# Slot experts fed by layers: two tiles cleared late on other engines, domain weights normalized ahead, two dense tiles fetched last, low parts by halves

## The chip, the cores and the metric

One NeuronCore of a Trainium2 chip runs the whole program. The metric is device time of one execution in microseconds (us), the median of three runs. Five engines work beside each other, each with its own in-order queue: PE (TensorE, matrix products), DVE (VectorE), ACT (ScalarE), POOL (GpSimd) and SP (SyncE), which here only issues DMA transfers. An instruction waits on semaphores for what it needs, and everything behind it in the same queue waits with it.

## What is computed

Three stages, one after the other. Inputs and outputs are float32; B, H, S, D = 4, 8, 576, 64; x has 2304 rows of 512.

```python
def _attn_ref(q, k, v, f):
    scores = scale * np.matmul(q, k.transpose(0, 1, 3, 2))
    cum = np.cumsum(np.log(np.clip(f, 0.0001, 1.0)), axis=-1)
    scores = np.where(causal, -1e9, scores + cum[:, :, :, None] - cum[:, :, None, :])
    attn = softmax(scores)                       # over the last axis
    return np.matmul(attn, v)

def _moe_ref(x, phi, w1, w2):                    # 8 experts of 4 slots
    logits = x @ phi
    d = softmax(logits, axis=0); c = softmax(logits, axis=1)
    slot_input = d.T @ x
    for e in range(E):
        slot_out[e] = np.maximum(slot_input[e] @ w1[e], 0.0) @ w2[e]
    return c @ slot_out

def _moe2_ref(x, domain_probs, w1, w2):          # 4 dense experts, 512 -> 1024 -> 512
    p = domain_probs / (domain_probs.sum(-1, keepdims=True) + 1e-09)
    for e in range(E):
        out += p[:, e:e + 1] * (np.maximum(x @ w1[e], 0.0) @ w2[e])
    return out
```

## The kernel before, in words

**Stages.** Attention and the sums of the slot softmax run to about 212 us of the trace. Then come the eight slot experts in two layers: layer 1 (L762) for all experts, layer 2 (L787) expert by expert into one PSUM tile `so_ps`, with the last expert done in two halves of 256 columns (`layer2_last`, L797 and L799). Then `so_t`, the transposed slot output (L982, L983), is multiplied with the first dense layer of expert 0 (`g_make`, L959, split into a high part `gh` and a low part `gl` at L965 and L966), is spread over the slots (L872, L873), and from there the dense stage begins: for each of 36 blocks (4 experts x 9 pairs of row tiles), PE combines 512 hidden values with `c4t` (L887), ACT and DVE build the pieces `q`, `a` and sums `S`, and PE multiplies them with the second layer. Block m=0 does this directly (L1079). The other 35 blocks (L1059) use a Strassen scheme with seven products in place of eight.

**High and low parts.** Products in the dense stage are made from a rounded high part and a low part. The weights of one expert are four blocks B00, B10, B01, B11 and four sums T1 to T4 of them (L733). Each has a high part, cast by ACT (L746, `w_hi`), and a low part, the difference of the source and the high part (L752, `w_lo`), by POOL or DVE. Each is 128x1024, in four pieces of 256 columns; `0:2` and `2:4` name the halves. The pieces S have low parts too (L953, on POOL). The products of PE use them in the order high x high, low x high, high x low.

**Queues.** In attention a scheduler places the instructions. From the slot experts on, the order of PE, ACT, DVE and POOL is the order in which the code is written (`manual_schedule`). The order of the dense stage's preparations for expert 0 stands in the table `PRE0`, keyed by block and step. SP's queue carries all loads in one order (`load_w` takes the next of a list `stream`); eight transfers are in flight, since a transfer waits for the one eight before it. A weight tile is 128x1024 float32, 512 KB. The second dense layer of expert 0 is a buffer of four such tiles, called `ring` (`load_ring`); the four tiles of its first layer are called `m`, the slot experts' tiles `w`.

**Small tiles that the change touches.** `own` is a mask of ones (expert's own slots), used at L778; `si_f` holds the slot inputs, filled at L665; both are cleared by POOL at L168 to L170, when the program starts. `dpr` holds the domain probabilities, loaded by SP at L834; DVE normalizes it into `dpn` at L1019 to L1022, through `dps` (128x18), right behind the pieces of block m=0. `sel` (128x1024, a selector) is cleared and filled by POOL at L844 and L848. `c4_rep` (L694 to L697) makes for each of five `b` a rounded copy `chi`, a spread copy and a difference of `cn`, all on POOL. `orow` are the two halves of the last rows of `so_ps`, copied by ACT at L976.

Of the kernel before, what the change touches and what calls it, by code (L numbers as in the profile page):

```python
# [34 lines left out]
def soft_moe_kernel(tc, a, out):  # L35
# [12 lines left out]
    with ExitStack() as top:  # L48
# [104 lines left out]
        own = tl.tile([128, E1 * 36], F32, name="own")  # L153
# [405 lines left out]
        load_w(ex.enter_context(tc.tile_pool(name="post", bufs=6)), 6)  # L559

# [12 lines left out]
        with tc.manual_schedule(engines={E.PE, E.Activation, E.DVE}):  # L573
# [56 lines left out]
            dnat(B - 1)  # L630
            busy(1)
# [37 lines left out]
            pool.tensor_tensor(cn[:, B - 1], ce, cs[:, :, None].to_broadcast([128, 5, 32]), op=ALU.mult)  # L669

# [16 lines left out]
        c4_ps = {}  # L687

        def c4_rep(b):
# [3 lines left out]
            chi = c4p.tile([r, 4, 32], F32R, tag="chi", bufs=2, name=f"chi_{b}")  # L693
            pool.tensor_scalar(chi, src, 1.0, 1.0, op0=ALU.mult, op1=ALU.mult)  # L694
            two_of = lambda x: x[:, :, None, :].to_broadcast([r, 4, 2, 32])
            pool.tensor_scalar(c4[:, :, 0:4:2], two_of(f32(chi)), 1.0, 1.0, op0=ALU.mult, op1=ALU.mult)
            pool.tensor_tensor(c4[:, :, 1:4:2], two_of(src), two_of(f32(chi)), op=ALU.subtract)  # L697
            c4_ps[b] = c4

# [105 lines left out]
        for e in range(E1):  # L805
# [462 lines left out]
```

## Time and profile before

| quantity | value |
|---|---|
| median of three runs | 665.27 us (664.82 to 665.33) |
| the profiled execution, its own time | 666.66 us |
| span of its trace | 664.9 us |
| PE busy | 651.0 us, 98% of the span |
| DVE, ACT, POOL busy | 495.5, 348.8, 424.0 us (75%, 52%, 64%) |
| mean DMA rate over the span | 115 GB/s |

The span is what the trace covers of the profiled execution; 1.76 us of its time lie outside. In the page's strip of 40 slices (16.6 us each) PE has a 7 in the first slice and an 8 in the last and otherwise nines, with a few eights in the first third; the strip of the granted TensorE clock has one 7, in the slice from 266 to 283 us, and nines around it. So PE does almost nothing but work, and what can be looked for are the places where it waits, and what the clock does behind them. The engines beside it have a quarter and more of their time free, but the average says nothing on a given stage.

### The profile page before, as it was taken

What the parts mean: (1) busy time and instruction counts of PE and PEld (TensorE: products, weight loads), DVE (VectorE), ACT (ScalarE), POOL (GpSimd) and SP (SyncE); (2) the same over time, 40 slices, a digit from 0 to 9 for tenths busy, and PEclk for the clock granted to TensorE, in tenths of its full rate; (3) what the DMA queues carried; (4) which work ended last, traced back from release to release, by engine and by line L of the source; (5) the groups of instructions that cost most, each with busy time, mean ns of one, the idle gap of its engine ahead of it and who ended that gap; (6) DMA issues with size and microseconds to landing.
All of it is one profiled execution on the core that took longest, in us unless ns stands there. A gap on an engine that the chain in (4) does not pass through costs nothing.

```text
span 664.9 us, 15324 instructions
## 1 busy us (share of the span) xinstructions
PE 651.0 (98%) x5646; PEld 583.4 (88%) x5646; DVE 495.5 (75%) x1332; ACT 348.8 (52%) x840; POOL 424.0 (64%) x402
## 2 busy tenths in 40 slices
PE   7999999999999989899999999999999999999998
PEld 4778778788787439899999999999999999999997
DVE  6888889889884147867678876778876778876774
ACT  6778767777771135333547343447443446443441
POOL 5777767777641199453889663789753589835443
PEclk8999999999999999799999999999999999999999
DMA  5778687686247980303000303000303000011111
GB/s 167 227 219 252 187 271 219 205 275 184 85 166 303 414 334 1 127 1 129 1 1 1 128 1 127 2 0 2 128 1 128 1 1 2 33 48 48 52 45 64
DMA packets 27509, 76.15 MB, mean 115 GB/s; under 512 B 4014, under 2 KB 4654, under 8 KB 27436
## 3 DMA queue, kind: packets, MB, share of 16 engines
q1 hardware_dynamic: 27436, 75.18, 33.1%
q8 instruction: 45, 0.74, 0.5%
q14 instruction: 28, 0.23, 0.1%
HBM read 70.31 MB, written 4.72 MB: 113 GB/s over the span
## 4 chain that ended last, share of the span: by engine, by line
PE 86%; DVE 6%; DMA 4%; ACT 2%; issue 2%; DVEq 0%; ACTq 0%; SPq 0%
PE R L1059 28%; PE Q L1059 14%; PE P L1059 7%; PE pt L273 5%; PE avb L290 5%; PE two L887 5%; PE sc L240 3%; PE sc L237 3%; PE sc L224 3%; PE pl L342 2%; PE ava L302 2%; PE pt L264 2%; DMA m<-in_m 1%; DMA w<-in_w 1%; DVE dps L1020 1%
## 5 line engine op out<-in xcount | busy, mean ns | idle before, releaser
L953 POOL TENSOR_TENSOR s<-S,s 128x512 fp32r<-128x512 f32 x140 | 179.8, 1318 | 141.7 <-ACT s L949 141.7
L949 ACT CAST s<-S 128x512 fp32r<-128x512 f32 x140 | 77.1, 619 | 96.0 <-PE Q L1059 52.0
L214 ACT ACTIVATE p<-p,nm 128x256 f32<-128x256 f32 (+2 forms) x144 | 83.4, 580 | 28.4 <-DVE nm L210 27.1
L1059 PE MATMUL R<-wh_T,s 128*128 128x256 f32 x560 | 89.2, 281 | 0.6 <-DVE acc L1042 0.6
L1042 DVE SCALAR_TENSOR_TENSOR acc<-R,dpn,acc 128x256 f32<-128x256 f32 x116 | 56.0, 482 | 37.4 <-PE R L1059 34.2
L919 ACT ACTIVATE a<-two 128x256 f32<-128x256 f32 x70 | 26.9, 384 | 97.5 <-PE two L887 97.0
L1059 PEld LDWEIGHTS R<-wh_T,s 128*128 128x128 f32 x560 | 75.9, 188 | 1.4 <-ACT a L928 1.1
L210 DVE CUSTOM_DVE_ANT_0 p<-sc,maskb 128x256 f32<-128x256 f32 (+2 forms) x144 | 67.1, 489 | 4.2 <-PE sc L224 1.4
L945 DVE SCALAR_TENSOR_TENSOR S<-two,S 128x256 f32<-128x256 f32 x140 | 58.9, 420 | 3.6 <-POOL s L953 1.1
L945 DVE SCALAR_TENSOR_TENSOR S<-two,a 128x256 f32<-128x256 f32 x140 | 58.1, 415 | 0.0
L191 POOL TENSOR_TENSOR opd<-raw,opd 64x576 fp32r<-64x576 f32 x29 | 42.6, 1468 | 14.4 <-ACT opd L176 13.3
L237 PE MATMUL sc<-opd 128*128 128x256 f32 (+3 forms) x128 | 47.0, 377 | 1.6 <-ACT opd L509 1.6
L1059 PE MATMUL R<-wh_B,a 128*128 128x256 f32 x280 | 45.3, 284 | 3.1 <-DVE acc L1040 3.1
L935 DVE SCALAR_TENSOR_TENSOR q<-two,q 128x512 fp32r<-128x512 f32 x70 | 47.7, 681 | 0.0
L273 PE MATMUL pt<-ident,p 128*128 128x128 f32 x285 | 46.7, 282 | 0.5 <-DVE ptb L178 0.5
L887 PE MATMUL two<-c4t,gs 128*128 128x256 f32 x288 | 46.9, 286 | 0.0
L1059 PE MATMUL P<-wh_B,q 128*128 128x256 f32 x280 | 45.1, 283 | 0.0
L1059 PE MATMUL R<-wh_T,q 128*128 128x256 f32 x280 | 44.8, 282 | 0.0
L1059 PE MATMUL Q<-wh_T,s 128*128 128x256 f32 x280 | 44.4, 280 | 0.0
L1059 PE MATMUL R<-wl_T,s 128*128 128x256 f32 x280 | 44.3, 280 | 0.0
L1059 PE MATMUL Q<-wh_B,s 128*128 128x256 f32 x280 | 44.3, 280 | 0.0
L273 PEld LDWEIGHTS pt<-ident,p 128*128 128x128 f32 x285 | 32.1, 143 | 13.7 <-issue 10.3
(272 smaller groups left out, 1641.5 us busy)
## 6 DMA issues: line engine op xcount, KB each, us to landing
w<-in_w SPq DMA_DIRECT2D x54, 512.0 KB
ring<-in_m SPq DMA_DIRECT2D x28, 512.0 KB
raw<-in_k SPq DMA_DIRECT2D x64, 144.0 KB
v<-in_v SPq DMA_DIRECT2D x16, 320.0 KB
out<-acc SPq DMA_DIRECT2D x17, 256.0 KB
raw<-in_q SPq DMA_DIRECT2D x28, 144.0 KB
ring<-in_w SPq DMA_DIRECT2D x4, 512.0 KB
w_opd<-in_w SPq DMA_DIRECT2D x4, 512.0 KB
```

Source lines behind the costliest of these rows:

```text
L191: (dve if h == 0 else pool).tensor_tensor(lo, r, f32(hi), op=ALU.subtract)
L210: dve.tensor_tensor_reduce(out=pt_in[j][:, k0:k0 + n], in0=sc, in1=maskb[:, m0:m0 + n], scale=-SCALE, scalar=nm, op0=ALU.add, op1=ALU.min, ...
L214: act.activation(p, p, AF.Exp, bias=nm, scale=-1.0, accum_out=sums)
L237: pe.matmul(o, lhsT=qa[hh][:, qs], rhs=ka[hh][:, 0:n], start=True, stop=False)
L273: pe.transpose(t[:, i, :], pt_in[j][:, 128 * i:128 * i + 128], ident)
L887: pe.matmul(t[:, j, k], lhsT=gs[e][:, 128 * fc:128 * fc + 128], rhs=c4t[:, nb * BLK:nb * BLK + BLK])
L935: dve.scalar_tensor_tensor(o[:, 1], i, 0.0, f32(o[:, 0]), op0=ALU.max, op1=ALU.subtract)
L945: dve.scalar_tensor_tensor(sv[m, name][:, c], half[m, h][:, :, k, 128 * t:128 * t + 128], 0.0, other, op0=ALU.max, op1=op)
L949: act.copy(tile_of(m, name)[:, 0], sv[m, name])
L953: (eng or pool).tensor_tensor(o[:, 1], sv[m, name], f32(o[:, 0]), op=ALU.subtract)
L1042: dve.scalar_tensor_tensor(o, t, pcol, o, op0=ALU.mult, op1=ALU.add)
L1059: pe.matmul(t, lhsT=a[:, c, :], rhs=w[:, c, :], start=first and x == 0 and c == 0, stop=x == 2 and c == 3, skip_group_check=True)
```

## The change

1. `si_f` is cleared by ACT, at the end of the softmax (L632 of the changed kernel), and `own` (now bfloat16) by DVE behind L670, rather than both by POOL at the start.
2. `dpn` is loaded during attention and normalized in place, at L672 to L675, between the slot softmax and the slot experts, rather than inside block m=0.
3. The tiles of the second dense layer of expert 0 are no longer fetched together ahead of the last slot experts' tiles: two (chunks 0 and 2, which hold the halves 0:2) keep their place, the other two (chunks 1 and 3) go last, behind the four `m` tiles.
4. The high and low parts of B00 to B11 and T1 to T4 are made by halves: `0:2` as soon as the first two tiles are there, `2:4` later (partly between the steps of blocks 0 and 1, table `PRE0`). All low parts are POOL's now; DVE's four are gone.
5. `sel` is cleared and filled by ACT, and ACT makes the two copies of `c4_rep`; POOL keeps the difference (`c4_low`).

The diff, cut to its core:

```diff
-        pool.memset(own, 0.0)
-        pool.memset(own.rearrange("p (e x) -> p e x", x=36)[:, :, 0:4], 1.0)
-        pool.memset(si_f, 0.0)
...
+        sp.dma_start(out=dpn, in_=a["dp"])
...
             dnat(B - 1)
+            act.activation(si_f, ident[:, 0:1].to_broadcast([128, E1 * 132]), AF.Copy, scale=0.0)
...
             dve.reciprocal(cs, cs)
             pool.tensor_tensor(cn[:, B - 1], ce, cs[:, :, None].to_broadcast([128, 5, 32]), op=ALU.mult)
+            dve.tensor_reduce(dps, dpn, axis=AX.X, op=ALU.add)
+            dve.tensor_scalar(dps, dps, 1e-9, None, op0=ALU.add)
+            dve.reciprocal(dps, dps)
+            dve.tensor_tensor(dpn, dpn, dps[:, :, None].to_broadcast([128, 18, E2]), op=ALU.mult)
+            dve.memset(own, 0.0)
+            dve.memset(own.rearrange("p (e x) -> p e x", x=36)[:, :, 0:4], 1.0)
...
-            chi = c4p.tile([r, 4, 32], F32R, tag="chi", bufs=2, name=f"chi_{b}")
-            pool.tensor_scalar(chi, src, 1.0, 1.0, op0=ALU.mult, op1=ALU.mult)
+            chi = c4p.tile([r, 4, 32], F32R, tag="chi", bufs=5, name=f"chi_{b}")
+            act.copy(chi, src)
...
-            pool.tensor_scalar(c4[:, :, 0:4:2], two_of(f32(chi)), 1.0, 1.0, op0=ALU.mult, op1=ALU.mult)
-            pool.tensor_tensor(c4[:, :, 1:4:2], two_of(src), two_of(f32(chi)), op=ALU.subtract)
+            act.copy(c4[:, :, 0:4:2], two_of(f32(chi)))
...
+            c4_in[b] = (c4[:, :, 1:4:2], two_of(src), two_of(f32(chi)))
+        def c4_low(b):
+            pool.tensor_tensor(*c4_in[b], op=ALU.subtract)
...
             if e == 0:
-                raws[0] = load_ring(stream.index(("m2", 0, 0)))
+                raws[0] = ring.tile([128, 4096], F32, tag="w", name="ring_m2")
+                for i in (0, 2):
+                    load_w(raws[0][:, 1024 * i:1024 * i + 1024], 1, stream.index(("m2", 0, i)))
             elif e < 6:
                 load_w(ringb[0], 4 if e < 5 else 1)
+            if e == 5:
+                for i in (1, 3):
+                    load_w(raws[0][:, 1024 * i:1024 * i + 1024])
...
-            w_sum(0, x, 2, 4)
-        pool.memset(f32(sel), 0.0)
+        for x in ("B00", "B10", "B01", "B11"):
+            w_hi(0, x, act, 0, 2)
+            w_lo(0, x, pool, 0, 2)
+        slots(5)
+        layer2(5)
+        w_hi(0, "T2", act, 0, 2)
+        w_hi(0, "T1", act, 0, 2)
+        for b in (0, 1, 2, 3, B):
+            c4_rep(b)
+        act.activation(sel, ident[:, None, None, 0:1].to_broadcast([128, 4, 2, 128]), AF.Copy, scale=0.0)
         for jq in range(4):
             for i in range(2):
...
-        w_hi(0, "B00", act)
-        w_hi(0, "B10", act)
-        w_lo(0, "B00", dve, 0, 2)
-        slots(5)
-        layer2(5)
-        w_hi(0, "B01", act)
-        w_hi(0, "B11", act)
-        w_hi(0, "T2", act)
-        w_hi(0, "T1", act)
-        for b in (0, 1, 2, 3, B):
-            c4_rep(b)
-        w_lo(0, "B00", dve, 2, 4)
+        c4_low(0)
+        w_sum(0, "T3", 0, 2)
+        w_sum(0, "T4", 0, 2)
...
         slots(6)
-        w_lo(0, "B10", dve, 0, 2)
         slots(7)
-        w_lo(0, "B10", dve, 2, 4)
...
+        w_hi(0, "B00", act, 2, 4)
+        w_lo(0, "B00", pool, 2, 4)
...
-        dve.tensor_reduce(dps, dpr, axis=AX.X, op=ALU.add)
-        dve.tensor_scalar(dps, dps, 1e-9, None, op0=ALU.add)
-        dve.reciprocal(dps, dps)
-        dve.tensor_tensor(dpn, dpr, dps[:, :, None].to_broadcast([128, 18, E2]), op=ALU.mult)
...
+        PRE0 = {(0, 0): [("hi", "B01", "a", 2, 4), ("lo", "B01", "p", 2, 4)],
```

What the diff doesn't tell is how the queues read afterwards. In the rows of an order the first word is the line of that kernel, then operation, tiles (out<-in) and size.

SP's queue of loads, before: the four ring tiles together, then the w tiles of the last slot experts (`w2`, left out in part), then the m tiles (`m1`), then the probabilities.

```order
L73 DMA w2_4_2_3250<-in_w2 128x1024
L73 DMA ring_45_3284<-in_m2 128x1024 x4
L73 DMA w2_4_3_3305<-in_w2 128x1024
L73 DMA w2_5_0_3307<-in_w2 128x1024
...
L73 DMA w2_7_3_3379<-in_w2 128x1024
L73 DMA m1_0_0_3381<-in_m1 128x1024
L73 DMA m1_0_1_3383<-in_m1 128x1024
L73 DMA m1_0_2_3385<-in_m1 128x1024
L73 DMA m1_0_3_3409<-in_m1 128x1024
L834 DMA dpr_3507<-in_dp 128x72
```

SP's queue there now:

```order
L73 DMA w2_4_2_3258<-in_w2 128x1024
L73 DMA ring_m2_3292<-in_m2 128x1024 x2
L73 DMA w2_4_3_3311<-in_w2 128x1024
L73 DMA w2_5_0_3313<-in_w2 128x1024
...
L73 DMA w2_7_3_3385<-in_w2 128x1024
L73 DMA m1_0_0_3387<-in_m1 128x1024
L73 DMA m1_0_1_3389<-in_m1 128x1024
L73 DMA m1_0_2_3391<-in_m1 128x1024
L73 DMA m1_0_3_3415<-in_m1 128x1024
L73 DMA ring_m2_3292<-in_m2 128x1024 x2
```

Each w and m tile stands two transfers further ahead, and two ring tiles stand at the end.

DVE's queue where block m=0 ends and block m=1 begins, before: the four operations on `dps` and `dpn` stand between the pieces `q` and the sums `S`.

```order
L898 SCALAR_TENSOR_TENSOR q1_0_3713<-two1_3260,q1_0_3713 128x512
L898 SCALAR_TENSOR_TENSOR q2_0_3716<-two1_3260,q2_0_3716 128x512
L1019 TENSOR_REDUCE dps_3508<-dpr_3507 128x18
L1020 TENSOR_SCALAR dps_3508<-dps_3508 128x18
L1021 RECIPROCAL dps_3508<-dps_3508 128x18
L1022 TENSOR_TENSOR dpn_3505<-dpr_3507,dps_3508 128x72
L945 SCALAR_TENSOR_TENSOR S1_1_3818<-two0_3259,a21_1_0_3794 128x256
L945 SCALAR_TENSOR_TENSOR S2_1_3820<-two0_3259,S1_1_3818 128x256
```

They stand now at the end of the slot softmax, ahead of the slot experts:

```order
L667 TENSOR_TENSOR si_f_132<-maskb_97,busy_2_3194 128x8x2x4
L669 TENSOR_SCALAR cs_e_3199<-cs_e_3199 128x5
L670 RECIPROCAL cs_e_3199<-cs_e_3199 128x5
L672 TENSOR_REDUCE dps_135<-dpn_134 128x18
L673 TENSOR_SCALAR dps_135<-dps_135 128x18
L674 RECIPROCAL dps_135<-dps_135 128x18
L675 TENSOR_TENSOR dpn_134<-dpn_134,dps_135 128x72
L676 MEMSET own_133 128x144
L677 MEMSET own_133 128x8x4
```

Behind the `q` of block m=0 the sums `S` follow at once.

POOL's queue in blocks 0 and 1 now, from the second halves on (before, L752 and L733 stood there for whole blocks, and two of the eight low parts were made by DVE):

```order
L763 TENSOR_TENSOR wl_0_B11_3544<-ring_m2_3292,wh_0_B11_3543 128x512
L744 TENSOR_TENSOR T1_0_3527<-ring_m2_3292 128x512
L744 TENSOR_TENSOR T2_0_3529<-T1_0_3527,ring_m2_3292 128x512
L744 TENSOR_TENSOR ring_m2_3292<-ring_m2_3292 128x2x256
L744 TENSOR_TENSOR ring_m2_3292<-ring_m2_3292,T2_0_3529 128x2x256
L763 TENSOR_TENSOR wl_0_T2_3558<-T2_0_3529,wh_0_T2_3557 128x512
L763 TENSOR_TENSOR wl_0_T1_3561<-T1_0_3527,wh_0_T1_3560 128x512
L968 TENSOR_TENSOR s0_1_3912<-S2_1_3828,s0_1_3912 128x512
L968 TENSOR_TENSOR s0_1_3912<-S1_1_3826,s0_1_3912 128x512
L763 TENSOR_TENSOR wl_0_T3_3618<-ring_m2_3292,wh_0_T3_3617 128x512
L968 TENSOR_TENSOR s1_1_3937<-S3_1_3849,s1_1_3937 128x512
L968 TENSOR_TENSOR s1_1_3937<-S4_1_3851,s1_1_3937 128x512
```

The low parts of block 1's sums (`s0_1`, `s1_1`) now stand behind the second halves of all weights. The order of loads and of POOL's work inside attention also differs, by some places, since the scheduler placed it anew with two memsets less; PE's order there is the same.

## Rows read from the trace of the kernel before

**Rows 1.** Waits of PE, whole span: us in total, times, longest.

```profile
PE R L1059 <- DVE acc L1040: 3.1, 1, 3.1
PE two L797 <- DMA w<-in_w: 1.8, 3, 0.6
...
PE two L959 <- DMA m<-in_m: 0.5, 1, 0.5
...
PE sc L240 <- DMA opd<-opd: 0.3, 1, 0.3
```

**Rows 2.** Windows: us, busy of PE, PEld, DVE, ACT, POOL (count), granted clock, DMA share, GB/s.

```profile
212.00:226.00 14.00, 13.94 (x251) 8.19 (x254) 0.86 (x3) 0.38 (x1) 0.45 (x1) 1.00 0.88 349
...
238.00:248.00 10.00, 7.71 (x88) 3.36 (x80) 1.84 (x5) 1.23 (x3) 9.44 (x20) 1.00 0.83 335
...
252.40:265.00 12.60, 12.56 (x106) 12.36 (x104) 11.23 (x6) 6.52 (x13) 12.60 (x11) 1.00 0.00 1
265.00:268.00 3.00, 0.00 (x0) 0.00 (x0) 2.90 (x10) 0.00 (x0) 0.15 (x1) 0.88 0.00 0
268.00:272.00 4.00, 3.92 (x18) 3.95 (x19) 3.97 (x10) 2.18 (x5) 1.48 (x2) 0.50 0.02 4
272.00:275.00 3.00, 3.00 (x20) 3.00 (x19) 1.13 (x4) 1.04 (x3) 3.00 (x3) 0.65 0.26 57
```

**Rows 3.** DVE's timeline: start us, us, line, operation; in brackets the idle time before.

```profile
211.91 0.19 DVE L668 RECIPROCAL cs_e<-cs_e 128x5 f32<-128x5 f32 x1
...
232.83 1.29 DVE L752 TENSOR_TENSOR wl_B<-ring,wh_B 128x512 fp32r<-128x512 f32 x1
...
236.17 0.68 DVE L752 TENSOR_TENSOR wl_B<-ring,wh_B 128x512 fp32r<-128x512 f32 x1
...
243.46 0.42 DVE L799 TENSOR_TENSOR orow<-orow,two 128x256 f32<-128x256 f32 x1 [4.91 <-PE two L797]
...
248.40 0.42 DVE L965 CAST gh<-two 128x256 fp32r<-128x256 f32 x1 [2.54 <-PE two L959]
...
256.39 8.79 DVE L1020 TENSOR_SCALAR dps<-dps 128x18 f32<-128x18 f32 x1
```

**Rows 4.** POOL's timeline, same columns.

```profile
229.81 2.52 POOL L733 TENSOR_TENSOR T<-ring 128x512 f32<-128x512 f32 x2 [17.11 <-PE so_ps L787]
...
236.25 2.90 POOL L848 TENSOR_SCALAR sel<-i 32x64 fp32r<-32x64 f32 x8
...
239.99 0.73 POOL L697 TENSOR_TENSOR c<-cn,chi 128x256 f32<-128x256 f32 x1
...
256.39 5.03 POOL L752 TENSOR_TENSOR wl_T<-T,wh_T 128x512 fp32r<-128x512 f32 x4
261.38 3.77 POOL L752 TENSOR_TENSOR wl_T<-ring,wh_T 128x512 fp32r<-128x512 f32 x3
```

**Rows 5.** PE's timeline from the last slot expert to the dense stage.

```profile
241.46 0.63 PE L797 MATMUL two<-w,ht 128*32 128x256 f32 x4 [0.61 <-DMA w<-in_w]
242.71 1.49 PE L797 MATMUL two<-w,ht 128*32 128x256 f32 x20 [0.62 <-DMA w<-in_w]
244.13 0.63 PE L982 MATMUL two<-i,orow 128*128 128x32 f32 x4
...
245.53 1.66 PE L959 MATMUL two<-m,so_t 128*32 128x256 f32 x24
247.69 0.64 PE L959 MATMUL two<-m,so_t 128*32 128x256 f32 x8 [0.51 <-DMA m<-in_m]
```

**Rows 6.** Chain of waits, 222 to 247 us: start us, us, what.

```profile
237.73 9.92 DMA m<-in_m
```

**Rows 7.** ACT's timeline, 226 to 249 us.

```profile
231.48 3.89 ACT L746 CAST wh_B<-ring 128x1024 fp32r<-128x1024 f32 x4 [4.38 <-DMA w<-in_w]
235.81 2.00 ACT L746 CAST wh_T<-T 128x1024 fp32r<-128x1024 f32 x2 [0.44 <-issue]
239.29 0.65 ACT L976 COPY orow<-so_ps 128x256 f32<-128x256 f32 x2 [1.48 <-PE so_ps L787]
```

More of the change, by code (lines that the diff above doesn't have):

```diff
@@ L152, in soft_moe_kernel @@
         si_f = tl.tile([128, E1 * 132], F32, name="si_f")
-        own = tl.tile([128, E1 * 36], F32, name="own")
+        own = tl.tile([128, E1 * 36], BF16, name="own")
+        dpn = tl.tile([128, 18, E2], F32, name="dpn")
+        dps = tl.tile([128, 18], F32, name="dps")
+        tl.tile([128, 46], F32, name="pad")
         si_t = si_f.rearrange("p (e x) -> p e x", x=132)[:, :, 0:128].rearrange("p e (c y) -> p e c y", y=32)[:, :, :, 0:4]
@@ L685, in soft_moe_kernel @@
         ops = top.enter_context(tc.tile_pool(name="ops", bufs=4, space=PSUM))
-        c4_ps = {}
+        c4_ps, c4_in = {}, {}
         def c4_rep(b):
@@ L829, in soft_moe_kernel @@
         so_t = c4tp.tile([128, DC, 32], F32, name="so_t")
-        dpn = c4tp.tile([128, 18, E2], F32, name="dpn")
         sel = c4tp.tile([128, 4, 2, 128], F32R, name="sel")
-        dpr = c4tp.tile([128, 18, E2], F32, name="dpr")
-        dps = c4tp.tile([128, 18], F32, name="dps")
-        sp.dma_start(out=dpr, in_=a["dp"])
+        c4tp.tile([128, 8], F32, name="pad2")
         gsp = top.enter_context(tc.tile_pool(name="gsp", bufs=2, side="right"))
@@ L847, in soft_moe_kernel @@
                 r = slice(32 * jq, 32 * jq + 32)
-                pool.tensor_scalar(sel[r, jq, i, 64 * i:64 * i + 64].rearrange("p (a s) -> p a s", a=2),
-                                   i4[r, None, :].to_broadcast([32, 2, 32]), 1.0, 1.0, op0=ALU.mult,
-                                   op1=ALU.mult)
-        w_hi(0, "B00", act)
-        w_hi(0, "B10", act)
-        w_lo(0, "B00", dve, 0, 2)
-        slots(5)
-        layer2(5)
-        w_hi(0, "B01", act)
-        w_hi(0, "B11", act)
-        w_hi(0, "T2", act)
-        w_hi(0, "T1", act)
-        for b in (0, 1, 2, 3, B):
-            c4_rep(b)
-        w_lo(0, "B00", dve, 2, 4)
+                act.copy(sel[r, jq, i, 64 * i:64 * i + 64].rearrange("p (a s) -> p a s", a=2),
+                         i4[r, None, :].to_broadcast([32, 2, 32]))
+        c4_low(0)
+        w_sum(0, "T3", 0, 2)
+        w_sum(0, "T4", 0, 2)
+        c4_low(1)
+        c4_low(2)
+        w_lo(0, "T2", pool, 0, 2)
+        c4_low(3)
+        c4_low(B)
+        w_lo(0, "T1", pool, 0, 2)
         slots(6)
-        w_lo(0, "B10", dve, 0, 2)
         slots(7)
-        w_lo(0, "B10", dve, 2, 4)
         def g_spread(e, gh, gl, hf):
@@ L976, in soft_moe_kernel @@
             act.copy(orow[h], so_ps[:, 256 * h:256 * h + 256])
+        for x in ("T3", "T4"):
+            w_hi(0, x, act, 0, 2)
+            w_lo(0, x, pool, 0, 2)
         for h in range(2):
@@ L991, in soft_moe_kernel @@
             c4_hi(b)
-        for x in ("B01", "B11"):
-            w_lo(0, x, pool, 0, 2)
-            w_lo(0, x, pool, 2, 4)
-        for x in ("T3", "T4"):
-            w_sum(0, x, 0, 2)
-            w_sum(0, x, 2, 4)
         attn.close()
@@ L1003, in soft_moe_kernel @@
             g_spread(0, *gg, hf)
+        w_hi(0, "B10", act, 2, 4)
+        w_lo(0, "B10", pool, 2, 4)
         c4_tr(3, c4_bank(3))
@@ L1097, in soft_moe_kernel @@
                (9, 4): [("lo", "B11", "p", 2, 4), ("lo", "T4", "d", 0, 2)], (9, 5): [("lo", "T4", "p", 2, 4)]}
-        PRE0 = {(0, 0): [("lo", "T2", "p", 0, 2)], (0, 1): [("hi", "T3", "a", 0, 4), ("lo", "T2", "p", 2, 4)],
[3 rows of a table removed]
+        PRE0 = {(0, 0): [("hi", "B01", "a", 2, 4), ("lo", "B01", "p", 2, 4)],
[6 rows of a table added]
         ENG = {"a": act, "d": dve, "p": pool}
```

9 rows, old and new, of the table PRE0 are left out of this document.

## The prediction, on record before the changed kernel ran

> **What bounds the kernel now.** I read PE's waits over the whole span first [rows 1]. PE is busy for 98% of it, and what it waits for by name is small, with two exceptions: once 3.1 us for DVE (L1040), and 1.8 + 0.5 us for DMA of the slot experts' tiles w and of the dense tiles m. Both lie between 238 and 275 us, so the windows of that stretch come next [rows 2]. The reader is to see three things there. From 238 to 248 PE works 7.71 of 10 us. From 265 to 268 it does nothing. Behind that its granted clock is 0.50 (the 1.2 GHz level) for 4 us and 0.65 on average for 3 more, while it is busy throughout: work goes on at half speed.
>
> The DMA wait is read from PE's timeline [rows 5]: L797 starts at 241.46 and 242.71 as w tiles land, 1.24 us apart, and L959 waits once more for the last m tile, which lands at 237.73 + 9.92 = 247.65 [rows 6]. All transfers stand in one stream at its full rate, so the order in the queue decides what lands when.
>
> The DVE wait is read from its timeline [rows 3]: the tensor_scalar on `dps`, 18 numbers a partition, takes 8.79 us, 256.39 to 265.18, where the reciprocal of five numbers takes 0.19. Beside it POOL runs seven low parts without a gap and ends at 261.38 + 3.77 = 265.15 [rows 4]. DVE is let go when POOL stops. The sums S and the copies to `acc` of block m=0 stand behind it on DVE; PE needs those banks, and waits 3.1 us.
>
> **The change part by part.**
>
> *dps out of block m=0.* The loss is the idle time and what the lower clock cost. Of the 10 us from 265 to 275, PE did work worth 4 x 0.50 + 3 x 0.65 = 3.95 us at full clock [rows 2], so 6.05 us are lost. Afterwards q of block m=0 ends at about 256.2 on DVE, S follows at once, and nothing that I see is late before PE gets there: at most 3 us of DVE work stand between q and the start of block m=1. Gain 6.05, if nothing else takes the place (rival 1). The four operations now run at about 212.1, behind the reciprocal that ends there [rows 3]. POOL runs one instruction of 0.45 us in that whole stage [rows 2]; even shut out by it they end near 213.3, as do the two clears of `own`, whose first reader is layer 2. PE enters layer 1 on `si_f` and its own products, both ahead of them. Cost nothing; without that cover it would be about 1 us.
>
> Here a page bears on it. The Trainium skill, SBUF — State Buffer, section "Who interferes with whom", says that DVE and POOL share a port pair as an exclusive lock held for one whole instruction, and that DVE needs it in a 2-port mode or with two inputs in SBUF. That agrees with a tensor_scalar that can't run beside POOL; but by that rule it would wait for one POOL instruction, 5.03 / 4 = 1.26 us, dps would not be what is late, and the time would be that of rival 3. The trace shows it shut out for seven in a row [rows 3, 4], and the row decides.
>
> *Ring order.* Two tiles fewer stand ahead of each w and m tile: 2 x 1.24 = 2.48 us earlier. The last w tile lands at 240.23 rather than 242.71, the last m tile at 245.17; the two late ring tiles at 246.4 and 247.65. That would be worth 2.48 us if nothing else came last.
>
> *What is late next: ACT.* `layer2_last` adds to `orow`, which ACT copies from `so_ps`; before, ACT was free and did so at 239.29 [rows 7]. Now it has ahead of this: four casts 128x512 from 231.48, two more from 235.81 (when T1, T2 and the queue allow it in the trace of before), five pairs of `chi` and c4 copies, the clear of `sel` and eight small copies. From rows: 3.89 / 4 = 0.97 for 1024 columns and 0.65 / 2 = 0.33 for 256 give 0.5 to 0.55 for 512, 0.3 for each of the ten copies, 0.97 to 1.05 for the clear. That is 236.9 behind T1 and T2, 240.0 behind the copies, 241.0 behind the clear; for the eight 32x64 copies I take 0.17 each (0.33 less 192 columns at (0.97 - 0.33) / 768 a column; bounds, as estimates, 0.15 and 0.25), so 242.3, and `orow` at 242.6, bounds 242.1 and 243.4. DVE's add then starts at 242.6 rather than 243.46 [rows 3]. From there as before: L982 0.67 later, L959 1.40 after that [rows 5], so 244.67. Its 32 products, now uninterrupted because m has landed up to the last eight, take (1.66 - 0.17) + (0.64 - 0.17) = 1.96 us, 0.17 being the drain that stands in each row. `gh` starts at 246.8 against 248.40 [rows 3]: gain 1.6. Bounds: 0.8 with the late end of ACT, 2.48 where only DMA decides. PE then idles in one piece, about 241.7 to 243.3; in before, four waits of 0.5 to 0.6 left the clock at 1.00 [rows 2], and I take it to hold (rival 2).
>
> *Low parts by halves.* POOL is now the busy one: from 229.81 [rows 4] T1, T2, then all low parts 0:2, the five differences of 0.73, then the second halves. With 1.26 for each half I get B10's second half at 251, then a wait on ACT for B01's high half, B01 256.4, B11 258, the four sums 263, T2 264.2, T1 265.5, and block 1's own low parts: S2 266.7, S1 268.0, T3 269.2, S3 270.5, S4 271.7, T4 273.0. PE now starts block m=0 at 250.7 and, 12.6 us later, block m=1 at 263.3; at 0.118 us a product (12.56 / 106) it reaches the first low part of S2 36 products later, at 267.6. Margins counted in this way for those six: 0.9, 1.0, 1.4, 0.4, 0.6, 0.5 us. Cost nothing, but the cover is thin: a POOL half of 1.32 in place of 1.26 over 24 of them takes 1.4 us and leaves PE about 1 us late. In exchange DVE loses four low parts, of 0.68 to 1.29 us [rows 3], which PE did not wait for.
>
> *The rest.* POOL's clears at the start: its next instruction waits for a load, no gain. `si_f` on ACT takes about 1.0 us (0.97 for 1024 columns [rows 7]) in the tail of the softmax and must end before DVE fills `si_f`, just ahead of the reciprocal at 211.91; by my count it has over 1 us of room, and it can cost 1.0 at most. The `sel` work, 2.90 us and more on POOL [rows 4], is what the ACT chain above pays. Attention: the same loads, some places apart. Before, PE waited there for a copy `opd` once, 0.3 us [rows 1]. I take 0, bounds -0.4 and +0.5.
>
> **Sum.** -6.05 - 1.6 = -7.65. Against the profiled execution: 666.66 - 7.65 = 659.0, span 657.25. That execution is 1.39 above the median of the three runs; from the median, 657.6 us.
>
> **The rivals.**
>
> *1. POOL or ACT becomes the bound in blocks 0 to 2.* For: margins of 0.4 to 0.9 us behind some 40 us of unbroken POOL work, and casts of ACT that wait in order for the late ring tiles, ahead of `gs` and `q`. Against: PE late moves its own deadlines, so lateness is paid once. Price: 1 to 2.5 us idle, and up to 3 us of lower clock behind it, as at 268 to 275. Time 659.5 to 663.
>
> *2. The clock falls behind the one piece of idle time at 242.* For: 3.1 us in one piece did it. Against: this is half as long, and the sum of waits there is smaller than before. Price 2 to 3 us, time 660 to 661.
>
> *3. dps isn't what is late,* or the stall moves to another DVE operation: only the DMA part is left, or nothing. Time 663.7 to 665.3. Against: `q`, S and acc stand behind dps without a gap, and all DVE operations in POOL's new long stretch take an input from PSUM, as did those that ran at 0.42 beside POOL at 243.46.
>
> *4. Slower: the loads in attention.* SP issues in order, and the new order puts the 31 small copies of `opd` behind other loads than before; several now wait for a slot of the eight. Each one late holds the next group of scores on PE. One place cost 0.3 us before. It decides against the change when the 31 are late by 0.25 us on average (7.7 in all); at 0.4 the time is 670. Against: PE has 98% there, with one such wait in 31.
>
> *5. DMA alone decides after all* (ACT faster than I count): 656.8.
>
> **How the numbers follow.** Forecast as above, 656.0 to 659.5: 0.62. Rivals 1 and 2 together, 659.5 to 663: 0.20. Rival 5: 0.06. Rival 3: 0.05, of which two fifths within 0.2%. Rival 4: 0.07, of which one within 0.2% and six slower. The range 655.8 to 662.8 takes in the forecast, rival 5, the bounds of ACT and attention and most of rivals 1 and 2, which leaves out some 0.15. About 0.2%, 1.3 us, is what a measurement of this kernel tells from no change. Faster: 0.62 + 0.20 + 0.06 + 0.03 = 0.91; same 0.03; slower 0.06.
>
> **What would show it.** Right: L1040's wait gone from PE's waits, the granted clock 1.00 from 248 to 280, dps near 0.2 to 0.6 us at 212, `gh` near 246.8, the second row of waits at L797 down to one, on ACT or DVE rather than DMA. Wrong: waits at L1059 on POOL's low parts in blocks 1 and 2, a granted clock under 1 behind 243, L240 on `opd` several times, or `gh` moved and the end not.

## The result, and the profile after

The changed kernel takes 656.67 us (median of four runs, 655.94 to 658.35) where the kernel before takes 665.3 (664.82 to 666.04): ratio 0.9873, 95% interval 0.985 to 0.9895, or 8.6 us less. The prediction said 657.6, between 655.8 and 662.8. The time came out as forecast, but in good part by other terms than those of its sum, as this section and the runs below show.

The profiled execution took 658.35 us, span 656.6, against 666.66 and 664.9. The waits of PE over the span (us in total, times, longest), to be laid beside [rows 1]:

```profile
PE two L1000 <- DVE orow L810: 1.9, 1, 1.9
PE Q L1071 <- DVE acc L1052: 1.4, 1, 1.4
...
PE two L808 <- DMA w<-in_w: 0.2, 1, 0.2
```

The wait of 3.1 us for DVE is gone, and those for w and m tiles nearly so. Behind attention two others have come: 1.9 us for `orow`, and 1.4 us for an accumulation on DVE. The windows (columns as in [rows 2]):

```profile
238.00:248.00 10.00, 8.12 (x69) 5.06 (x62) 1.95 (x6) 5.20 (x15) 9.05 (x10) 0.68 0.57 231
...
252.40:265.00 12.60, 12.60 (x110) 12.60 (x109) 8.19 (x19) 8.75 (x20) 8.64 (x7) 1.00 0.01 2
265.00:268.00 3.00, 3.00 (x29) 3.00 (x28) 1.20 (x3) 2.04 (x5) 3.00 (x4) 1.00 0.00 0
268.00:272.00 4.00, 4.00 (x33) 3.72 (x32) 2.00 (x5) 1.15 (x3) 4.00 (x4) 1.00 0.00 0
272.00:275.00 3.00, 1.56 (x14) 1.39 (x13) 2.20 (x6) 0.00 (x0) 1.95 (x2) 1.00 0.05 8
```

From 252 to 272 PE now works without a break at full clock, where before it stood still at 265 and then ran at 0.50 and 0.65. But the stretch from 238 to 248 has a granted clock of 0.68, where it was 1.00, and PE works only 1.56 of 3 us from 272 on.

Where the 8.3 us of the span come from is seen by placing five marks in the timelines of all executions: the second filling of `si_f` on DVE (the end of attention and softmax), the start of `gh`, the first product of block m=0, the 230th last accumulation on DVE (the second of block m=3), and the last one. Times between them, in us:

| execution | to `si_f` | to `gh` | to block 0 | to block 3 | to the end |
|---|---|---|---|---|---|
| before | 211.57 | 36.83 | 4.06 | 43.53 | 365.74 |
| after | 209.15 | 38.07 | 4.39 | 39.26 | 362.56 |
| difference | -2.42 | +1.24 | +0.33 | -4.27 | -3.18 |

So the part up to `si_f` gained 2.4 us that nobody had forecast, the stage around the last slot expert lost 1.2 where 1.6 was to be gained, blocks 0 to 2 gained 4.3 in place of 6.05, and the long rest, in which no instruction had changed, gained 3.2.

### The profile page after: what moved, and what is told of

It reads as the page before. It is cut to its first block, busy times and chain, and to the rows that moved or that the text cites. A ratio compares the mean times of both kernels' runs of the same rounds, so it can differ in the third digit from the quotient of the medians.

```text
span 656.6 us, 15328 instructions
## 1 busy us (share of the span) xinstructions
PE 644.6 (98%) x5646; PEld 576.4 (88%) x5646; DVE 482.5 (73%) x1330; ACT 355.8 (54%) x868; POOL 420.0 (64%) x384
## 4 chain that ended last, share of the span: by engine, by line
PE 85%; ACT 4%; DVE 3%; POOL 3%; issue 2%; DMA 2%; ACTq 0%; DVEq 0%; POOLq 0%
PE R L1071 27%; PE Q L1071 13%; PE P L1071 7%; PE avb L290 5%; PE pt L273 5%; PE two L902 5%; PE sc L240 3%; PE sc L237 3%; PE sc L224 3%; PE pl L342 2%; PE ava L302 2%; PE pt L264 2%; DMA w<-in_w 2%; PE two L974 1%; PE nat L317 1%
```

## The experiments

All times are medians, beside runs of the kernel before on the same chip; the ratio is to that kernel, with its 95% interval. The table continues the one above, from the profiled execution of each.

| run | time, us | ratio | to `si_f` | to `gh` | to block 0 | to block 3 | to the end |
|---|---|---|---|---|---|---|---|
| before_dps | 658.41 | 0.9881 (0.9857 to 0.9904) | 212.82 | 36.71 | 4.05 | 37.25 | 362.77 |
| undo_dps | 655.99 | 0.9843 (0.9829 to 0.9858) | 209.97 | 35.45 | 4.05 | 39.25 | 362.72 |
| undo_clear | 658.26 | 0.9880 (0.9865 to 0.9894) | 211.35 | 37.05 | 4.04 | 39.34 | 363.01 |
| before_clear | 663.72 | 0.9961 (0.9948 to 0.9974) | 209.54 | 36.94 | 4.05 | 42.49 | 365.73 |
| undo_ring | 658.06 | 0.9872 (0.9845 to 0.9898) | 210.57 | 36.75 | 4.06 | 39.33 | 363.00 |
| orow_first | 654.95 | 0.9827 (0.9814 to 0.9840) | 209.35 | 34.27 | 4.35 | 39.33 | 362.70 |
| after_again | 655.89 | 0.9847 (0.9829 to 0.9865) | 209.51 | 35.44 | 4.04 | 39.29 | 362.59 |
| both | 657.22 | 0.9862 (0.9839 to 0.9884) | 210.56 | 34.22 | 6.58 | 38.77 | 362.76 |
| mid_casts | 653.85 | 0.9811 (0.9794 to 0.9828) | 209.63 | 34.36 | 4.31 | 37.40 | 362.70 |
| pad_back | 661.10 | 0.9911 (0.9890 to 0.9931) | 209.80 | 37.07 | 4.04 | 39.38 | 365.83 |
| mid_casts_a | 655.89 | 0.9843 (0.9827 to 0.9859) | 209.84 | 34.24 | 4.32 | 37.46 | 365.46 |
| mid_casts_b | 653.53 | 0.9807 (0.9791 to 0.9823) | 209.48 | 34.27 | 4.37 | 37.44 | 362.72 |

### The dps stall: before_dps and undo_dps

before_dps makes only part 2 of the change in the kernel before (`own` becomes bfloat16, to make room):

```diff
+        sp.dma_start(out=dpn, in_=a["dp"])
...
             pool.tensor_tensor(cn[:, B - 1], ce, cs[:, :, None].to_broadcast([128, 5, 32]), op=ALU.mult)
+            dve.tensor_reduce(dps, dpn, axis=AX.X, op=ALU.add)
+            dve.tensor_scalar(dps, dps, 1e-9, None, op0=ALU.add)
+            dve.reciprocal(dps, dps)
+            dve.tensor_tensor(dpn, dpn, dps[:, :, None].to_broadcast([128, 18, E2]), op=ALU.mult)
...
-        dve.tensor_reduce(dps, dpr, axis=AX.X, op=ALU.add)
...
```

> The kernel before, with the domain weights normalized ahead of the slot experts and nothing else of the change. Theory A (the prediction's largest term): the tensor_scalar on dps takes 0.2 to 0.6 us at 212, PE's wait of 3.1 us for DVE (L1040) and the lower granted clock behind it go, 6.0 us less than before (about 659.3). Theory B (only part of that stall is dps; POOL's low parts of block 1 are next): 3.5 to 4.5 us less, with a new wait of 1 to 2 us for POOL's low parts around 270.

Block 0 to block 3 took 37.25 us in place of 43.53: 6.3 us, the forecast's 6.05 within 0.3, and no other wait came there. Its windows:

```profile
252.40:265.00 12.60, 12.60 (x109) 12.40 (x108) 7.66 (x18) 7.52 (x15) 12.60 (x11) 1.00 0.01 2
265.00:268.00 3.00, 3.00 (x28) 3.00 (x28) 1.64 (x4) 2.28 (x6) 3.00 (x4) 1.00 0.00 0
268.00:272.00 4.00, 4.00 (x37) 4.00 (x36) 2.57 (x7) 1.00 (x3) 4.00 (x4) 1.00 0.48 144
```

The idle time and the lower clock behind it are gone together, as theory A says. How much it is worth depends on how long the clock stays down: in before_clear, below, the same stall of 3.1 us was followed by 3.4 us of the lower clock rather than 6.8, and the stage took 42.49, which makes it 5.2. (The whole run gained 8.1 us by the medians. In the profiled execution 3.0 of it are the pace told of in the last section on runs, and 1.25 are lost in attention, where the loads had been placed anew, PE waited 0.9 us for a copy of `opd` at 20 us and the granted clock was 0.50 for 3.4 us behind it; which of these made the 1.25 wasn't tested.)

undo_dps puts the four operations of the changed kernel back behind the pieces of block m=0:

```diff
-            dve.tensor_tensor(dpn, dpn, dps[:, :, None].to_broadcast([128, 18, E2]), op=ALU.mult)
...
         cq.close()
+        dve.tensor_reduce(dps, dpn, axis=AX.X, op=ALU.add)
...
```

> The changed kernel with the four operations on dps and dpn put back behind the pieces of block m=0. Theory A (DVE is shut out as long as POOL runs without a gap): POOL now stands idle there until about 256.0, so the tensor_scalar takes about 0.2 to 0.8 us, and the time is within 1 us of the changed kernel's 656.7. Theory B (its place beside POOL's low parts decides, as the prediction has it): it waits 8 us or more, to the end of POOL's run, and 5 us or more are lost (661.7 or above).

DVE's timeline there:

```profile
253.41 0.18 DVE L1032 TENSOR_SCALAR dps<-dps 128x18 f32<-128x18 f32 x1
...
253.92 1.33 DVE L1034 TENSOR_TENSOR dpn<-dpn,dps 128x72 f32<-128x72 f32 x1
```

POOL's timeline at the same time:

```profile
253.87 1.29 POOL L759 TENSOR_TENSOR wl_B<-ring_m,wh_B 128x512 fp32r<-128x512 f32 x1 [4.21 <-ACT wh_B L753]
```

The same tensor_scalar takes 0.18 us at the same place in DVE's queue, because POOL happened to be idle (4.21 us, waiting for ACT); the next operation but one, with two inputs from SBUF, starts just as POOL does and takes 1.33 us, about as long as POOL's instruction. POOL then stood idle again for 0.26 us, so this row alone doesn't tell whether DVE waited for one instruction or for the end of POOL's run. POOL's timeline of the kernel before does:

```profile
232.28 2.98 POOL L733 TENSOR_TENSOR T<-T,ring 128x512 f32<-128x512 f32 x2
```

DVE's low part at 232.83, with two inputs from SBUF, took 1.29 us beside it and was done by 234.1 [rows 3], in the middle of POOL's run, and POOL's two instructions took 2.98 us, where the two ahead of them took 2.52 [rows 4]. Such an operation gets its turn between two of POOL's; the tensor_scalar did not.

Theory A holds: it is not the place in the program but POOL's run without a gap that shuts DVE out. In the changed kernel the move is therefore not even needed: undo_dps is as fast as after_again. In the kernel before, where POOL has no gap there, it is worth 5.2 to 6.3.

### The start: undo_clear and before_clear

```diff
+        pool.memset(own, 0.0)
+        pool.memset(own.rearrange("p (e x) -> p e x", x=36)[:, :, 0:4], 1.0)
+        pool.memset(si_f, 0.0)
...
-            act.activation(si_f, ident[:, 0:1].to_broadcast([128, E1 * 132]), AF.Copy, scale=0.0)
```

> The changed kernel with own and si_f cleared by POOL at the start again. Theory A (POOL's clears shut out DVE's first tensor_scalar, L494, and that delay is the first scores'): that operation is spread over 1.6 us rather than 0.5, the first scores start near 9.0 rather than 7.7, the granted clock falls to 0.50 around 12 to 16, and the time is 2.4 us above the changed kernel's (659.1). Theory B (the order of loads in attention is what changed the start, or the clears are hidden as the prediction has it): within 0.5 us.

The start of DVE's timeline in undo_clear:

```profile
3.53 1.47 DVE L497 TENSOR_SCALAR fr<-fr 64x256 f32<-64x256 f32 x2 [3.53 <-DMA fr<-in_f]
```

POOL's beside it:

```profile
3.42 0.34 POOL L171 MEMSET own<- 128x288 bf16 x1
3.70 1.13 POOL L173 MEMSET si_f<- 128x1056 f32 x1
4.77 0.30 POOL L172 MEMSET own<- 128x32 bf16 x1
```

DVE's in the changed kernel:

```profile
3.58 0.52 DVE L494 TENSOR_SCALAR fr<-fr 64x256 f32<-64x256 f32 x2 [3.58 <-DMA fr<-in_f]
```

The clip of `f` (two tensor_scalars, 0.52 us alone) lasts until about 5.0, when POOL's clears are nearly done. It is the first link to the first scores, which start at 8.5 rather than 7.7; and in the window from 12 to 16 the granted clock is 0.61, where it is 1.00 in the changed kernel. Undo_clear's windows of that stretch:

```profile
12.00:16.00 4.00, 4.00 (x23) 3.81 (x22) 2.50 (x9) 2.25 (x6) 2.88 (x4) 0.61 0.57 156
```

`si_f` comes at 211.35, as in the kernel before (211.57), 2.2 us later than in the changed kernel. That is theory A in kind, but not all of it is the clears. By the starts of the same products on PE's timeline undo_clear is 0.8 us behind the changed kernel at the first scores and 1.5 at 25 us; the last 0.7 come at 66 us, where PE waits 0.6 us for a copy of `opd`, and so belong to the order of the loads. Nor is the lower clock tied to the clears: undo_ring and mid_casts_a, which clear late, show 0.68 and 0.69 in the same window and lost 0.8 and 0.6 us by 25 us. The medians, 658.26 and 656.67, have intervals that overlap; the reading rests on the timelines and on before_clear.

before_clear does the reverse: the same three clears moved, in the kernel before, and nothing else.

> The kernel before with own and si_f cleared late (DVE and ACT) and nothing else of the change. Theory A: DVE's L494 is done by 4.2 rather than 5.1, the first scores start 1.3 us earlier, the granted clock doesn't fall around 12 to 16, and the time is 2.0 to 2.6 us less than before (663.0 by the first median, 664.2 by the second). Theory B (the start is hidden): within 0.5 us of before.

0.39% less (0.26 to 0.52), 2.3 us by the medians, and `si_f` 2.0 us earlier. The first scores start at 7.75 rather than 8.99, and the granted clock doesn't fall there: theory A. By the same products 1.8 of the 2.0 are there at 25 us. In both kernels the order of loads in attention follows along, since the scheduler counts the clears, so the two are not parted further on; but the tensor_scalar at the start shows the delay directly, and every profiled execution with the clears on POOL reaches `si_f` at 211.3 or later, every other at 210.6 or earlier.

### The last slot expert: undo_ring, orow_first and after_again

undo_ring fetches all four ring tiles together again:

```diff
-                raws[0] = ring.tile([128, 4096], F32, tag="w", name="ring_m2")
-                for i in (0, 2):
-                    load_w(raws[0][:, 1024 * i:1024 * i + 1024], 1, stream.index(("m2", 0, i)))
+                raws[0] = load_ring(stream.index(("m2", 0, 0)))
...
-            if e == 5:
-                for i in (1, 3):
-                    load_w(raws[0][:, 1024 * i:1024 * i + 1024])
```

> The changed kernel with all four tiles of the second dense layer of expert 0 fetched together again, ahead of the last w tiles. Theory A (in the changed kernel ACT, not DMA, is last at orow, so the earlier w and m tiles bring nothing there): the last w tile lands at about 240.3, the wait of 1.9 us in one piece is cut in several of 0.5 to 0.9, gh at about 246.0, between the 245.4 of the changed kernel without and its 247.2 with a fall of the clock; the time within 1 us of 656.7. Theory B (the order of the tiles is worth its 1.6 to 2.5 us as forecast): gh 1.6 us or more later than 245.4, 1.6 us lost or more against executions of the changed kernel without a fall of the clock.

PE's waits are those of before again [rows 1]:

```profile
PE two L808 <- DMA w<-in_w: 1.7, 3, 0.6
```

`si_f` to `gh` takes 36.75, as before (36.83). The time, 658.06, can't decide: its interval overlaps those of the changed kernel in both runs. after_again is the changed kernel, run once more:

> The changed kernel once more, beside the others on the same chip. Theory A (whether the granted clock falls behind the 1.9 us of idle time before gh differs from one execution to the next, as between the changed kernel, pad_back and undo_dps so far): gh at 245 to 247.5, times spread by 2 us or more, 656 without a fall, 657 to 658.5 with one. Theory B (the fall belongs to the kernel): gh near 247.2 and times within 0.5 us of each other.

There the same wait of 2.0 us for `orow` stood ahead of `gh`, and the clock did not fall. `g_make` (L974) on PE's timeline in the first execution:

```profile
241.19 0.79 PE L1000 MATMUL two<-i,orow 128*128 128x32 f32 x4 [1.88 <-DVE orow L810]
...
243.51 3.64 PE L974 MATMUL two<-m,so_t 128*32 128x256 f32 x32
```

And in this one:

```profile
241.55 0.63 PE L1000 MATMUL two<-i,orow 128*128 128x32 f32 x4 [1.98 <-DVE orow L810]
...
242.95 1.93 PE L974 MATMUL two<-m,so_t 128*32 128x256 f32 x32
```

32 products take 3.64 us in one (granted clock 0.50, the 1.2 GHz level, from about 241.5 to past 248), 1.93 in the other, and the stage is 38.07 or 35.44 us long. So the tile order is worth 36.75 - 35.44 = 1.3 us where the clock stays (theory B of undo_ring in kind; it asked for 1.6 to 2.5), and costs 0.2 to 1.2 where it falls. It fell in the profiled executions of the changed kernel (for 6.8 us), undo_clear and pad_back (for 3.4 us, the stage 37.05 and 37.07 us long) and not in undo_dps and after_again, with idle times of 1.8 to 2.1 us in all: it differs from one execution to the next, and nothing in these traces tells which. The nine timed runs of the changed kernel agree: six with a mean granted clock of 1.000 took 655.69 to 656.11 us, two with 0.997 took 657.23 and 657.43, the one with 0.995 took 658.35. By the trace theory A of after_again holds; its spread, 1.7 us in five runs, is a little less than it asked for.

orow_first takes away the cause of the idle time, ACT's queue ahead of `orow`. In the changed kernel ACT comes to `orow` only behind `sel`:

```profile
237.62 1.05 ACT L865 ACTIVATE sel<-ident 128x1024 fp32r<-128x1024 f32 x1
238.70 1.58 ACT L869 CAST sel<-i 32x64 fp32r<-32x64 f32 x8
240.30 0.65 ACT L991 COPY orow<-so_ps 128x256 f32<-128x256 f32 x2
```

And DVE adds to `orow` when ACT has copied it:

```profile
240.71 0.76 DVE L810 TENSOR_TENSOR orow<-orow,two 128x256 f32<-128x256 f32 x2 [5.19 <-ACT orow L991]
```

The edit:

```diff
-        act.activation(sel, ident[:, None, None, 0:1].to_broadcast([128, 4, 2, 128]), AF.Copy, scale=0.0)
...
             act.copy(orow[h], so_ps[:, 256 * h:256 * h + 256])
+        act.activation(sel, ident[:, None, None, 0:1].to_broadcast([128, 4, 2, 128]), AF.Copy, scale=0.0)
```

> The changed kernel with ACT's two copies to orow ahead of the clear and the filling of sel. Theory A (ACT's queue ahead of orow makes the idle time of 1.9 us at 239 to 241, and that makes the lower clock behind it): orow ready about 2.6 us earlier, the granted clock 1.00 throughout, gh at about 243.6 to 244.5 rather than 247.2, and the time 2.5 to 3.5 us less (653.2 to 654.2), less a wait for POOL in blocks 1 and 2 that may grow from 1.4 by 1. Theory B (POOL and ACT in blocks 0 and 1 set the time whatever comes before): gh as in A, but the time within 1 us of 656.7, with waits for POOL larger by what was gained.

The wait for `orow` is gone and PE waits at `gh` for DMA, 0.5 us, as before; the stage takes 34.27 us, 2.56 less than before: the 2.48 that two tiles are worth. All of it reached the end: blocks 0 to 2 took 39.33, as in the changed kernel. The time is 654.95, with its four runs between 654.91 and 655.67. `gh` at 243.62 is theory A's; the time is only 1.7 below the changed kernel's 656.67, less than the 2.5 to 3.5 of theory A, and neither theory has it. The expectation was reckoned from the execution in which the clock fell; against after_again's 35.44 the stage gains 1.2.

### POOL in blocks 0 and 1: both and mid_casts

POOL's timeline in the changed kernel; in brackets the idle time ahead of a row and for whom:

```profile
250.53 1.27 POOL L763 TENSOR_TENSOR wl_B<-ring_m,wh_B 128x512 fp32r<-128x512 f32 x1 [3.48 <-ACT wh_B L757]
256.02 1.29 POOL L763 TENSOR_TENSOR wl_B<-ring_m,wh_B 128x512 fp32r<-128x512 f32 x1 [4.21 <-ACT wh_B L757]
...
266.47 2.53 POOL L968 TENSOR_TENSOR s<-S,s 128x512 fp32r<-128x512 f32 x2
...
270.21 2.52 POOL L968 TENSOR_TENSOR s<-S,s 128x512 fp32r<-128x512 f32 x2
272.69 1.26 POOL L763 TENSOR_TENSOR wl_T<-ring_m,wh_T 128x512 fp32r<-128x512 f32 x1
```

DVE's, behind it:

```profile
271.53 0.42 DVE L960 SCALAR_TENSOR_TENSOR S<-two,a 128x256 f32<-128x256 f32 x1 [0.89 <-POOL s L968]
272.76 0.42 DVE L960 SCALAR_TENSOR_TENSOR S<-two,S 128x256 f32<-128x256 f32 x1 [0.81 <-POOL s L968]
273.10 0.48 DVE L1052 TENSOR_SCALAR acc<-Q,dpn 128x256 f32<-128x256 f32 x1
```

PE's wait of 1.4 us ends with the accumulation at 273.10. (The expectations place this wait at block 2; it falls in block 1, ahead of the sixth of its seven products.) The accumulation stood on DVE behind two sums S of block 2, and these waited for POOL to release the S tiles of block 1. POOL is late because it stood idle for 3.48 and 4.21 us, waiting for ACT's casts of B10 and B01, which ACT does behind `gs` and behind all `q`. Two runs give POOL these casts earlier. both (on orow_first) puts all of them ahead of the casts for c4t and gs:

```diff
-        w_hi(0, "B00", act, 2, 4)
-        w_lo(0, "B00", pool, 2, 4)
+        for x in ("B00", "B10", "B01", "B11"):
+            w_hi(0, x, act, 2, 4)
+            w_lo(0, x, pool, 2, 4)
```

> orow ahead of sel (as in orow_first) and, besides, the high and low parts 2:4 of B10, B01 and B11 right behind those of B00, ahead of ACT's casts for c4t and gs. Theory A (POOL is late in blocks 1 and 2 because it stands idle before, waiting for ACT's casts that stand behind q): POOL works on from 244 without the gaps, the wait of 1.4 us for DVE behind POOL at block 2 goes, and the time is 1.5 to 2 us below orow_first's 654.95 (653.0 to 653.5). Theory B (POOL's amount of work sets it, or the casts in front delay gs and q as much): within 0.5 us of orow_first.

The wait of PE that is new there:

```profile
PE two L896 <- ACT gs L176: 2.3, 1, 2.3
```

ACT's timeline ahead of it:

```profile
246.50 1.66 ACT L757 CAST wh_B<-ring_m 128x512 fp32r<-128x512 f32 x3 [0.61 <-DMA ring_m<-in_m]
248.07 1.06 ACT L719 CAST c4t<-ct 128x512 fp32r<-128x512 f32 x2
249.02 0.66 ACT L176 CAST gs<-two 128x256 fp32r<-128x256 f32 x2
```

The wait for the accumulation is gone, but the three casts wait for the last ring tile, which landed at 246.5 here, and `gs` waits behind them in ACT's queue: PE lost 2.3 us, with a granted clock under 1 behind. Neither theory had that: the run is 2.3 us slower than orow_first by the medians. Of the 2.9 us between the two profiled executions 2.2 were lost ahead of block 0 and 0.6 gained in blocks 0 to 2; another 1.2 were lost in attention, ahead of the edit, where PE waited 1.1 us for a load of `v`. mid_casts keeps B10 where it was and puts B01 and B11 between the pieces:

```diff
+        w_hi(0, "B01", act, 2, 4)
+        w_lo(0, "B01", pool, 2, 4)
         c4_tr(B, c4_bank(B))
...
+        w_hi(0, "B11", act, 2, 4)
+        w_lo(0, "B11", pool, 2, 4)
         c4_hi(3)
```

> orow ahead of sel, as in orow_first, and ACT's casts of the halves 2:4 of B01 and B11 (with POOL's low parts behind them) between ACT's pieces q of block m=0 rather than behind all of them and the next block's; unlike in the run called both, nothing new stands ahead of gs. Theory A (POOL's idle time before block 1, not its amount of work, makes the wait of 1.4 us at block 2): POOL makes B01's low part about 2.5 us earlier, the wait for DVE behind POOL at block 2 goes or falls under 0.3 us, and the time is 1.0 to 2.0 us below orow_first's (653.0 to 654.0). Theory B (casts put ahead of the second pair of q delay block 0 as much): within 0.5 us of orow_first (654.5 to 655.5) or above.

Its windows behind block 1:

```profile
268.00:272.00 4.00, 4.00 (x34) 3.83 (x33) 3.88 (x11) 1.70 (x4) 1.80 (x2) 1.00 0.49 155
272.00:275.00 3.00, 3.00 (x28) 3.00 (x28) 1.29 (x4) 1.76 (x4) 3.00 (x4) 1.00 1.04 422
```

No wait for the accumulation, 37.40 us from block 0 to block 3, 1.9 less than the changed kernel and as short as in before_dps. Theory A holds: POOL's idle time, not its amount of work, was the cause. The time is 653.85 us, 1.1 below orow_first (their intervals overlap) and, on the same chip, 2.0 below the changed kernel (after_again), ratio 0.9811 to before: faster than both kernels.

### The pace of the rest: pad_back, mid_casts_a and mid_casts_b

before_dps already showed the gain of 3 us behind block 3, so neither the low parts nor the tile order makes it. What it shares with the changed kernel is memory: with `dpr`, `dpn` and `dps` gone from the right-hand pool, c4t, gs, T1, T2 and the first four pairs of weight parts lie 640 bytes higher. pad_back moves them back by padding alone:

```diff
-        c4tp.tile([128, 8], F32, name="pad2")
+        c4tp.tile([128, 168], F32, name="pad2")
```

> The changed kernel with 640 bytes more of unused padding, so that c4t, gs, T1, T2 and the first four pairs of weight parts lie at the addresses that they had before; no instruction differs. Theory A (the faster pace of TensorE in experts 2 and 3, 115.6 ns a product rather than 117.8, comes from where these tiles lie): the pace goes back to 117.8 ns from 460 us on and the time is 3.0 us above the changed kernel's (about 659.7 by the median, 661.4 beside the profiled execution). Theory B (pace comes from the place of dpn or own, or from the chip of the day): pace 115.6 and the time of the changed kernel.

The window from 470 to 650 us in the changed kernel:

```profile
470.00:650.00 180.00, 179.76 (x1555) 177.90 (x1555) 135.09 (x315) 80.28 (x169) 107.90 (x84) 1.00 0.12 46
```

The same window in pad_back:

```profile
470.00:650.00 180.00, 179.82 (x1534) 178.26 (x1534) 133.98 (x313) 80.60 (x169) 107.56 (x84) 1.00 0.12 46
```

PE is busy and at full clock in both, but does 1555 products in one and 1534 in the other. The spacing of DVE's accumulations gives the time of a whole block of 92 products (84 with the second layer, 8 for the next block's pieces). Its median is 10.63 us in expert 2 and 10.70 in expert 3 in the changed kernel, or 115.6 and 116.3 ns a product, and 10.85 and 10.86 in pad_back, or 117.9 and 118.0, as in the kernel before. In expert 1 it is 10.78 against 10.87, and in expert 0 there is next to no difference (10.83 and 10.84). The end comes 3.27 us later behind the mark in block 3. Theory A: addresses alone make the difference. (The median time, 661.10, is 4.4 above the changed kernel's where 3.0 was expected; two of the six runs took 659.1 and 659.2, which is 3.0 to 3.5 above the changed kernel's runs at full clock. Of the other four, three show a mean granted clock of 0.995 to 0.997; the fourth, 661.18, shows 1.000, and why it is slow stays open.)

mid_casts_a and mid_casts_b are mid_casts with 320 and 1024 bytes more of the same padding.

> mid_casts with 320 bytes more of padding: c4t, gs, T1, T2 and the first four pairs of weight parts lie 320 bytes above their addresses of before, rather than 640; no instruction differs. Theory A (only some offsets between these tiles and the others are fast): the pace in experts 2 and 3 is between 115.3 and 118, and what it is decides whether 640 was a lucky value; 0 to 3 us above mid_casts. Theory B (what counts is only that the tiles don't lie at multiples of 4096 bytes, as before): 115.6 as with 640, time as mid_casts.

> mid_casts with 1024 bytes more of padding: the same tiles lie 384 bytes below their addresses of before. Theory A (only some offsets are fast): pace 117 to 118 in all experts, or another pattern than with 640; up to 3 us above mid_casts. Theory B (any place off the multiples of 4096 bytes is fast): 117.3 in experts 0 and 1, 115.6 in 2 and 3, time as mid_casts.

At 320 bytes above the old place the pace is that of before (10.86 us a block in expert 2, 10.85 in expert 3), and the time 2.0 us above mid_casts; at 384 below it, it is that of mid_casts (10.63 and 10.70), and the time 653.53, the same within the intervals. So not every place off the old one is fast, and theory A of mid_casts_a holds. mid_casts_b came out with the numbers of its theory B, but as a rule that theory is refuted by mid_casts_a. 640 and -384 differ by 1024. Whether that is the period, and which of the moved tiles counts against which other, stays open.

## Why the prediction came out right, step by step

**dps, 6.05.** Right as a term: 6.28 in before_dps, or 5.2 where the clock stays down half as long. What failed is "if nothing else takes the place" and, with it, the next step.

**Low parts by halves, cost nothing.** Wrong: 2.0 us (39.29 in place of 37.25 from block 0 to block 3). POOL's times were forecast well: counted from the start of block m=0, T4's low part is done after 22.3 us in both. The low parts reached PE in time but for one: laid beside before_dps product by product, PE loses 0.2 us at S3's high part, 0.2 at S3's low part, whose margin was put at 0.4, and 1.6 at the wait for the accumulation. The step left out the other reader of POOL's work: DVE's sums of the next block wait for the S tiles that POOL frees, and the accumulation that PE waits for stands behind them in DVE's queue. That was rival 1 in kind, with 1.4 us of idle time, near its lower end, and the clock held.

**Ring order and orow, 1.6.** Right in an execution in which the clock stays (1.4 by after_again against before: 35.44 and 36.83). ACT, not DMA, is last at `orow`, as forecast. DVE's add starts at 240.71; with the 2.4 us that `si_f` came earlier that is 243.1 against the forecast's 242.6, in part because the eight small copies took 0.20 us each rather than 0.17. Rival 2, the fall of the clock, came in the profiled execution and turned the gain into a loss of 1.2; the step that took the clock to hold was wrong for some executions. It was priced at 2 to 3 us and cost 2.6 there (38.07 against 35.44), and 1.6 in undo_clear and pad_back.

**The clears at the start, no gain.** Wrong: by 25 us of the trace they had cost 1.5 to 1.8 us (undo_clear, before_clear), and 2.0 between the two kernels, the lower clock included. The step looked only at POOL's own next instruction, which waits for a load. It didn't ask what DVE does beside the clears, although the dps row had just shown what POOL can do to a DVE tensor_scalar.

**Attention, -0.4 to +0.5.** It came out at the lower bound: behind the start the changed kernel gained another 0.4 us, most of it where before waited for a copy of `opd`. The bounds were narrow for such a change all the same: before_dps, with yet another order of loads, lost 1.25 in its profiled execution.

**Nothing said on the rest.** 3.2 us came from the addresses of unchanged tiles; no step had it.

So the sum of -7.65 against -8.3 in the span is right in part by luck, by errors that cancel: 2.4 + 3.2 came unforeseen, and against the forecast 2.8 were missing at the last slot expert (a gain of 1.6 became a loss of 1.2, by the clock), 1.8 in blocks 0 to 2 and 0.3 between them.

## What to carry to other kernels

Before a POOL instruction or a run of them is placed or removed, look at what DVE does beside it, and at the first microseconds as well as at the visible stall; and when a producer is made later, follow all its readers, the release of its buffers included. A change in a small tile's place moves every tile behind it: compare the pace of untouched stages before giving a gain to the edit, and test it with padding alone. Where an edit trades several short waits of PE for one long one, the granted clock can take back more than the order was worth (here 1.6 to 2.6 us against 1.3), in some executions and not in others.

## What the runs showed of the hardware

A DVE tensor_scalar on SBUF beside POOL was shut out for seven POOL instructions in a row (8.79 us before, 8.69 in before_clear) and by clears that only write (1.47 us for 0.52), and took 0.18 with POOL idle. A DVE tensor_tensor with two SBUF inputs waited for one POOL instruction (1.33 us in undo_dps) and got through in the middle of POOL's run (1.29 us before, at 232.83). The Trainium skill, SBUF — State Buffer, section "Who interferes with whom", has DVE and POOL exclude each other for a whole instruction. The traces agree with it for the tensor_tensor; for the tensor_scalar the measured 8.79 us decides: POOL's next instructions went ahead of the waiting one.

TensorE's pace at full granted clock depended on where its operands lie by 2.0% in expert 2 (115.6 and 117.9 ns a product, over whole blocks of the same 92 products).
